# Mamba-2 scan and SwiGLU: additions of the states moved behind the preceding outputs, mean squares by one product, root by ScalarE, dummy products in the lead-in

## The chip, the cores and the metric

The kernel runs on one core of a Trainium2 chip. The metric is the device time of one execution in microseconds; lower is better. The engines named below are TensorE (PE, with its weight loads as PEld), VectorE (DVE), ScalarE (ACT), GpSimd (POOL) and SyncE (SP), which only issues transfers. Each engine works through its own list of instructions in order and waits at semaphores where it needs another engine's result.

## What is computed

A state-space scan over 32 sequences (4 batches of 8 heads, 768 tokens, 32 channels, 16 states) in chunks, and then a gated feed-forward layer over the 3072 tokens it gives. Cut to what matters:

```python
for c in range(nc):                      # chunks of a sequence
    cum = np.cumsum(log_a[:, :, sl], axis=-1)
    L = np.exp(cum[..., :, None] - cum[..., None, :]) * causal
    y_intra = einsum('bhij,bhjd->bhid', einsum('bhin,bhjn->bhij', Cc, Bc) * L, xc)
    y_inter = einsum('bhin,bhnd->bhid', Cc, state) * np.exp(cum)[..., None]
    y[:, :, sl] = y_intra + y_inter
    state = decay_full * state + sum_j(Bc_j (x) xc_j * decay_from_j)
x = y as (tokens 3072, features 256)
xn = x / np.sqrt(np.mean(x * x, axis=-1, keepdims=True) + 1e-06) * rms_g
g, val = xn @ w_gate, xn @ w_val         # (3072, 1536) each
out = (g / (1 + np.exp(-g)) * val) @ w_out
```

The weights arrive as 64-bit floats and are turned into 32-bit ones on the chip.

## The kernel before

**Tiling.** The tokens are cut into six blocks of 512 (`TB`), each of two pairs of 128-token chunks; a chunk has two halves of 64, which are the chunks of the scan. The scan is done by pairs (12 of them, index p), the feed-forward layer by blocks. The feed-forward products of blocks 1 to 5, and of part of block 0, are done by Strassen's scheme with seven half-size products in place of eight: `P.1` to `P.7` for gate and value, `O.1` to `O.7` for the output projection, with sums and differences by VectorE.

**A pair of the scan.** `turn` transposes B, C and the decayed C on TensorE (L464), `T` and `Tt` take them out of PSUM by ScalarE; `g` forms the products of C and B (L494) in a pair of PSUM banks, and `L`, `L1` multiply them by the decays (L513, L519). `scale` makes Cd and Bd on VectorE (L449). `A` (`additions`, L534) forms what each half chunk adds to the state, in tiles of 64 rows by 32 columns of the array, in two single banks of its own. `S` (`states`, L547 to L557) multiplies these by a mask of heads and adds them to the decayed state. `y` (`outputs`, L574) forms the outputs: first from the states, then from the decayed products. The outputs lie in columns 0 to 127 of four banks: the two of a pair of banks and two single ones. `sq` (L610, L613) squares them, and `yt` (L624, L626) takes them out.

**The norm of a block.** `ms` (L636) forms the mean squares of 4 x 128 tokens by four products with a 128x32 matrix, each in its own column tile of the array. `mc` (L642, ScalarE) copies them out, `mt` (L645) transposes them, so that a token has a partition; `rs` adds 1e-6 on VectorE (L650) and raises to the power -0.5 on GpSimd (L652). `rb` (L658) spreads the roots over all partitions by four transposes, into a bank from which `xn` (L670, VectorE) multiplies them with the outputs and the gain. `tx` (L754) forms differences of xn for Strassen's scheme.

**The feed-forward of a block.** For each j of six: `P.k.j` (L777) is two products of 128x256, into a bank "gate" (k = 1, 4, 6, 7) or "val" (2, 3, 5). The products of gate accumulate in one bank, and `take` (L783, ScalarE) copies its state p out between them: product 6 has to wait for the copy after product 1, and 4 or 7 likewise. `C` (L789, VectorE) adds p to val, `silu` (L798, ScalarE) and `hid` (L802, VectorE) make the hidden values. `O.k.j` (L867) is two products of 128x128; the products 1, 6 and 7 share a bank, of which `Otake` (L883, ScalarE) copies the state v out after each of the three, so that `O.6` waits for the first copy and `O.7` for the second. `Oadd` (L894) adds up, `out` stores. `s`, `s2`, `s3`, `s4` (L833 to L843) are the sums of hidden values.

**PSUM.** Single banks have the tag "one" and are two; the pair of banks for g and y is one from block 1 on (slot 2), and there are two "gate" and two "val".

**Order.** The kernel's work stands in one long string of some 1600 steps, `block:step.numbers`, written out by hand or by a planner outside of the file; the program goes through it and issues each step's instructions, which thus stand in this order on each engine. Nothing in the kernel shifts them. A step of block b concerns the scan of the block after it, or the second after it for loads (`when`, `of_pair`). ScalarE evaluates only functions of the table set that is loaded, and a load of another set (ACT_TABLE_LOAD) is put in where the next function needs it: Silu in the feed-forward, Exp for the decays (`ex`, L434). SP's queue carries the loads, the weights and the stores, in the order of the string.

**Lead-in.** Block 0 starts with the loads, constants, twelve dummy products of 128x256 (`idle`, L274), the sums of logarithms (`r`, `d`, `c`), the first two pairs of the scan and the change of the weights to 32 bits, twenty pieces of them (`pow` by ScalarE, L169 to L172, `man` and `wt` by VectorE, L179 to L188). The first products of block 0 (`early`, L703) are done on outputs that aren't normed yet.

Of the kernel before, what the change touches and what calls it, by code (L numbers as in the profile page):

```python
# [20 lines left out]
def kernel(  # L21
# [60 lines left out]

    def bank(name, shape):
        return mm.tile(list(shape), FP32, tag="one", bufs=2, name=name)

    def pair_of_banks(name, slot):
        return (mm if slot == 2 else pairs[slot].pool).tile([P, 2, 512], FP32, tag="pair%d" % slot, name=name)
# [108 lines left out]
    zeros = const.tile([P, P], FP32, name="zeros")  # L196
# [15 lines left out]
    mean32 = const.tile([P, 32], FP32, name="mean32")  # L212
    nhalf = const.tile([P, NT], FP32, name="nhalf")
# [79 lines left out]
    def both_mids():  # L293
# [9 lines left out]
        "zeros": lambda: nc.vector.memset(zeros, 0.0),  # L303
        "upto": lambda: triangle(upto, ones, 0.0, 0, 1),
        "never": lambda: triangle(never, zeros, -2.0 ** 100, 0, 1),
# [9 lines left out]
        "kinks": kinks_of_powers, "mean32": lambda: nc.vector.memset(mean32, 1.0 / DM),  # L315
        "nhalf": lambda: nc.vector.memset(nhalf, -0.5),
# [212 lines left out]
    def additions(p):  # L529
        s = st[p]  # L530
        ps["A", p] = A_ps = [bank("A_ps", (P, 2, 2, D)) for u in range(2)]
        for i, u in chunks_of(p)[2]:
            for q in range(NQ):
                nc.tensor.matmul(  # L534
                    out=A_ps[u][32 * q:32 * q + 32, i].rearrange("p t d -> p (t d)"),
                    lhsT=s["Bd"][halves[u], i, 2 * q:2 * q + 2].rearrange("p t n -> p (t n)"),
                    rhs=s["x"][halves[u], i, 2 * q:2 * q + 2].rearrange("p t d -> p (t d)"),
                    start=(i == 0), stop=True, tile_position=(HC * u, 32 * q),
                    skip_group_check=True)
# [24 lines left out]
    def outputs(p, y):  # L564
# [25 lines left out]
        for i in range(2):  # L590
            for h in range(NH):
                for u in range(2):
                    o = 32 * (h % 4)
                    product_y(h // 4, u, i, slice(o, o + 32), lhsT=s["x"][halves[u], i, h],
                              rhs=Ls[p][halves[u], i, h], tile_position=(HC * u, o))
        del st[p], Ls[p]
# [35 lines left out]
    def norm_sums(blk):  # L632

        ps["m", blk] = ms = bank("ms", (P, 2, P))
        for k in range(NT):
            nc.tensor.matmul(out=ms[32 * k:32 * k + 32, 0], lhsT=mean32,  # L636
                             rhs=sqs[blk][:, k * P:(k + 1) * P], start=True, stop=True,
                             tile_position=(0, 32 * k), skip_group_check=True)

    def norm_out(blk):  # L640
        ps["mr", blk] = mr = nrm.tile([P, P], FP32, tag="r_sb", name="mr", bufs=2)
        nc.scalar.copy(out=mr, in_=ps["m", blk][:, 0])  # L642

    def norm_back(blk):
        nc.tensor.transpose(out=ps["m", blk][:, 1], in_=ps.pop(("mr", blk)), identity=ident)  # L645

    def norm_roots(blk):
        me = nrm.tile([P, NT], FP32, tag="me", name="me")
        ms = ps.pop(("m", blk))[:, 1].rearrange("p (k r) -> p k r", r=32)[:, :, 0]
        nc.vector.tensor_scalar_add(me, ms, 1e-6)  # L650
        ps["rs"] = rs = nrm.tile([P, NT], FP32, tag="rs", name="rs")
        nc.gpsimd.tensor_tensor(out=rs, in0=me, in1=nhalf, op=ALU.pow)  # L652

    def norm_turn():
        rs = ps.pop("rs")
        ps["rb"] = rb = bank("rb", (P, NT, P))
        for k in range(NT):
            nc.tensor.transpose(out=rb[:, k], in_=rs[:, k:k + 1].to_broadcast([P, P]),  # L658
                                identity=ident)

    def norm_copy():
        ps["r"] = r = nrm.tile([P, TB], FP32, tag="sq2", name="r", bufs=1)
        nc.scalar.copy(out=r, in_=ps["rb"].rearrange("p k m -> p (k m)"))

    def norm_apply(blk):
        rb = ps["rb"].rearrange("p k m -> p (k m)")
        xns[blk] = nrm.tile([P, 2, TB], FP32, tag="xn", name="xn", bufs=1)
        if blk:
            for t in range(2):
                nc.vector.scalar_tensor_tensor(out=xns[blk][:, t], in0=yts[blk][:, t],  # L670
                                               scalar=gcol[:, t:t + 1], in1=rb,
                                               op0=ALU.mult, op1=ALU.mult)
        else:
            nc.vector.tensor_tensor(out=xns[0], in0=yts[0],
                                    in1=rb.unsqueeze(1).to_broadcast([P, 2, TB]), op=ALU.mult)
# [34 lines left out]
    def normed(f):  # L710
        gv = ps.pop(("gv", f))
        us[f] = ffn.tile([P, TB], FP32, tag="u", name="u", bufs=2)
        for k, dst in enumerate((us[f], of_block_0(f))):
            nc.vector.tensor_tensor(out=dst, in0=gv[:, k], in1=ps["r"], op=ALU.mult)
# [254 lines left out]
    def by_vector(out, in_, scale):  # L969
# [23 lines left out]
        "ms": norm_sums, "mc": norm_out, "mt": norm_back, "rs": norm_roots, "rb": lambda b: norm_turn(), "rc": norm_copy, "xn": norm_apply,  # L993
# [26 lines left out]
    def of_chunk(n, fn):  # L1020
# [18 lines left out]
        "ms": when(1, norm_sums), "mc": when(1, norm_out), "mt": when(1, norm_back),  # L1039
        "rs": when(1, norm_roots),  # L1040
        "rb": when(1, lambda b: norm_turn()), "xn": when(1, norm_apply), "tx": when(1, combine_x),
# [5 lines left out]
        0:a 0:bc.0 0:kinks 0:nhalf 0:ident 0:set 0:bc.1 0:warm 0:idle.12 0:fetch.1 0:fetch.0 0:x.0  # L1047
        0:head 0:mean32 0:x.1 0:gcol 0:zeros 0:never 0:ones 0:upto 0:upto2 0:mid 0:mid2 0:after
        0:after2 0:fetch.3 0:fetch.6 0:part 0:fetch.2 0:fetch.5 0:fetch.4 0:mids 0:never16 0:bc.2
        0:fetch.8 0:aT 0:la0 0:log4.6.2 0:log4.0.4 0:log 0:r.0 0:d 0:whole 0:x.2 0:ident16  # L1050
        0:mask.0/2 0:fetch.7 0:log4.4.2 0:part2 0:sel 0:parts.0 0:c 0:dx 0:turn.0.1 0:T.0.1 0:sums.0
        0:fetch.9 0:hmask 0:cx 0:tmask 0:Tt.0.1.1 0:Tt.0.1.0 0:turn.0.0 0:Tt.0.0.1 0:T.0.0
        0:turn.1.1 0:exp.0 0:Tt.0.0.0 0:g.0/10 0:T.1.1 0:Tt.1.1.0 0:Tt.1.1.1 0:turn.1.0 0:Tt.1.0.1
        0:T.1.0 0:Tt.1.0.0 0:scale.0 0:last.0 0:Tl.0 0:bc.3 0:row.1 0:scale.1 0:mask.1/2 0:sums.1
        0:L.0.1 0:cc 0:pow.0 0:L.0.0 0:rowout.1 0:man.1 0:A.0 0:exp.1 0:S.0 0:g.1/01 0:A.1 0:pow.1
        0:L.1.0 0:mask.3/2 0:S.1 0:y.0/0 0:pow.3 0:wt.1 0:L.1.1 0:sq.0 0:yt.0 0:ydone.0 0:pow.2
        0:r.1 0:man.0 0:last.1 0:parts.1 0:Tl.1 0:pow.5 0:y.1/1 0:wt.0 0:man.2 0:early.0.0/0 0:man.3
        0:sq.1 0:yt.1 0:ydone.1 0:pow.4 0:sums.3 0:scale.2 0:turn.2.0 0:mask.2/1 0:ms.0 0:wt.2
        0:sums.2 0:wt.3 0:man.4 0:fetch.16 0:mc.0 0:mt.0 0:rs.0 0:man.5 0:fetch.10 0:wt.4
        0:early.0.1 0:wt.5 0:exp.2 0:man.6 0:T.2.0 0:Tt.2.0.1 0:Tt.2.0.0 0:exp.3 0:turn.2.1 0:T.2.1  # L1060
        0:Tt.2.1.0 0:Tt.2.1.1 0:rb.0 0:rc 0:xn.0 0:norm.0 0:pow.6 0:fetch.13 0:wt.6 0:early.1.0/1
        0:early.1.1 0:silu.0 0:gg.2/2 0:norm.1 0:x.5 0:L1.2.2 0:gate.2/0 0:pow.7 0:man.7 0:hid.0
        0:row.0 0:man.8 0:silu.2 0:gate.3/1 0:pow.8 0:rowout.0 0:hid.2 0:scale.3 0:turn.3.0 0:x.3
        0:L1.2.3 0:wt.7 0:gate.4/0 0:wt.8 0:man.9 0:man.10 0:pow.9 0:wt.9 0:silu.3 0:hid.3 0:cw.3
        0:gate.5/1 0:silu.1 0:T.3.0 0:Tt.3.0.0 0:Tt.3.0.1 0:A.2 0:pow.10 0:tx.0 0:silu.4 0:hid.4
        0:switch.0 0:P.1.3 0:fetch.11 0:man.11 0:pow.11 0:S.2 0:turn.3.1 0:wt.10 0:take.1.3 0:P.6.3
        0:wt.11 0:P.1.4 0:Tt.3.1.0 0:L.2.0 0:silu.5 0:hid.5 0:fetch.19 0:fetch.12 0:man.12 1:bc.0
        0:man.13 0:T.3.1 0:Tt.3.1.1 0:pow.12 0:y.2/2 0:sq.2 0:x.4 0:yt.2 0:ydone.2 0:switch.1
        0:P.2.4 0:P.2.3 0:wt.12 0:A.3 0:S.3 0:gg.3/2 0:L.3.0 0:fetch.14 0:take.1.4 0:spread.10
        0:take.6.3 0:P.7.3 0:pow.13 0:fetch.15 0:L1.3.2 0:L1.3.3 0:y.3/2 0:sq.3 0:yt.3 0:ydone.3  # L1070
        0:C.11.3 0:P.5.3 0:cw.4 0:C.11.4 0:P.6.4 0:take.7.3 0:wt.13 0:P.5.4 0:pow.14 0:C.22.3 0:ms.1
        0:man.14 0:P.3.3 0:P.4.3 0:C.12.3 0:silug.22.3 0:wt.14 0:tok 0:silug.12.3 0:P.2.5
        0:silug.21.3 0:hidg.22.3 0:hidg.21.3 0:mc.1 0:o.0/2 0:take.6.4 0:P.7.4 0:P.1.5 0:hid.1 0:o.1
        0:man.15 0:pow.15 0:cw.5 0:wt.15 0:o.2 1:spread.2 0:pow.16 0:mt.1 0:man.16 0:wt.16 0:o.3
        0:hidg.12.3 0:take.1.5 0:P.6.5 0:take.7.4 0:C.22.4 0:P.3.4 0:bc.5 1:scale.1 0:fetch.17
        0:pow.17 0:man.17 0:C.12.4 0:o.4 0:o.5 0:tokout 0:sub.10 0:take.6.5 0:P.7.5 0:rs.1 0:rb.1
        0:silug.11.3 0:hidg.11.3 0:C.11.5 0:P.5.5 1:two.0 0:fetch.18 0:pow.18 0:wt.17 0:silug.11.5
        0:silug.11.4 0:hidg.11.4 0:man.18 0:wt.18 0:take.7.5 0:P.4.5 0:C.22.5 0:silug.21.5 0:man.19
        0:silug.12.4 0:hidg.12.4 0:P.4.4 0:silug.21.4 0:hidg.21.4 0:silug.22.4 0:hidg.22.4 0:o.6
        0:o.7 0:pow.19 0:wt.19 0:P.3.5 0:C.12.5 0:silug.12.5 0:o.8 0:o.9 0:silug.22.5 0:xn.1 1:P.2.1  # L1080
        1:P.1.1 1:P.2.0 1:take.1.1 0:ex.10 0:hidg.11.5 0:hidg.21.5 1:P.1.0 0:hidg.12.5 0:hidg.22.5
# [166 lines left out]
```

## Time and profile before

| what | value |
|---|---|
| device time, three runs | 414.24, 414.83, 415.03 us, median 414.83 |
| profiled execution | 414.91 us, of which the span from its first to its last instruction is 413.2 |
| HBM | 20.02 MB read, 3.28 MB written |
| busy, 0 to 50 us | TensorE 49.9, VectorE 41.8, ScalarE 37.1, GpSimd 6.3 |
| busy, 50 to 100 us | 49.6, 44.4, 35.0, 2.7 |
| busy, 100 to 206 us | 105.6, 81.1, 57.6, 15.3 |
| busy, 206 to 300 us | 93.4, 63.2, 44.2, 15.4 |
| busy, 300 to 413.2 us | 110.5, 70.5, 40.9, 2.7 |

The profile is a page on one execution: shares of busy time, the span in 40 slices, transfers, the chain of work that ended last, and groups of equal instructions. A line of a group, or of the timeline, names the source line, the engine, the operation, what it writes and reads, and shapes as partitions x elements. A 32-bit product appears as two records of TensorE, a transpose as one. Records of TensorE overlap, so that the distance between starts, not the duration of a record, is what one costs in a stream.

### The profile page before, as it was taken

What the parts mean: (1) busy time and instruction counts of PE and PEld (TensorE: products, weight loads), DVE (VectorE), ACT (ScalarE), POOL (GpSimd) and SP (SyncE); (2) the same over time, 40 slices, a digit from 0 to 9 for tenths busy, and PEclk for the clock granted to TensorE, in tenths of its full rate; (3) what the DMA queues carried; (4) which work ended last, traced back from release to release, by engine and by line L of the source; (5) the groups of instructions that cost most, each with busy time, mean ns of one, the idle gap of its engine ahead of it and who ended that gap; (6) DMA issues with size and microseconds to landing.
All of it is one profiled execution on the core that took longest, in us unless ns stands there. A gap on an engine that the chain in (4) does not pass through costs nothing.

```text
span 413.2 us, 10058 instructions
## 1 busy us (share of the span) xinstructions
PE 403.3 (98%) x4118; PEld 343.2 (83%) x4118; DVE 301.0 (73%) x712; ACT 214.8 (52%) x497; POOL 42.3 (10%) x64
## 2 busy tenths in 40 slices
PE   7789999999999999999999999999999999999997
PEld 5457467888888899888899888899988889988897
DVE  5989999789968878476796465787366876356781
ACT  2869997755656426645362547451556431235410
POOL 2011000012300015000033000012200001000000
PEclk9989999999999999999999999999999999999999
DMA  9979848900111440201070406000100000100001
GB/s 121 255 157 238 208 53 173 203 0 2 39 39 52 92 65 27 78 0 29 12 85 10 78 2 127 2 2 2 52 0 3 1 3 0 52 0 2 1 2 51
DMA packets 87374, 23.95 MB, mean 58 GB/s; under 512 B 76800, under 2 KB 81152, under 8 KB 87328
## 3 DMA queue, kind: packets, MB, share of 16 engines
q1 hardware_dynamic: 83168, 23.05, 26.9%
q10 hardware_dynamic: 4160, 0.26, 1.1%
q8 instruction: 32, 0.52, 0.5%
q14 instruction: 14, 0.11, 0.1%
HBM read 20.02 MB, written 3.28 MB: 56 GB/s over the span
## 4 chain that ended last, share of the span: by engine, by line
PE 90%; DVE 6%; issue 2%; ACT 1%; POOL 0%; DVEq 0%; POOLq 0%
PE gate L777 27%; PE o L867 21%; PE val L777 20%; PE y L574 4%; PE gate L693 3%; PE o L809 3%; PE gate L703 2%; PE g L494 2%; PE tp L464 1%; PE A_ps L534 1%; DVE sw L747 1%; PE rb L658 1%; PE idle L274 1%; DVE L L428 1%; PE ms L636 1%
## 5 line engine op out<-in xcount | busy, mean ns | idle before, releaser
L789 DVE TENSOR_TENSOR c<-val,p 128x512 f32<-128x512 f32 x99 | 67.5, 688 | 41.8 <-PE val L777 33.4
L783 ACT COPY p<-gate 128x512 f32<-128x512 f32 x99 | 57.6, 588 | 69.5 <-PE gate L777 67.6
L777 PE MATMUL gate<-tx,sw 128*128 128x256 f32 x264 | 66.8, 383 | 0.7 <-ACT p L783 0.7
L777 PEld LDWEIGHTS gate<-tx,sw 128*128 128x128 f32 x264 | 48.6, 190 | 8.5 <-ACT p L783 1.4
L798 ACT ACTIVATE c<-c 128x256 f32<-128x256 f32 x99 | 38.4, 417 | 24.6 <-DVE c L789 24.5
L802 DVE TENSOR_TENSOR h<-c 128x256 f32<-128x256 f32 x99 | 41.2, 429 | 10.9 <-ACT c L798 10.9
L777 PE MATMUL val<-tx,sw 128*128 128x256 f32 x132 | 34.1, 383 | 0.4 <-DVE c L789 0.4
L777 PE MATMUL val<-xn,wgv 128*128 128x256 f32 x132 | 33.7, 381 | 0.0
L777 PE MATMUL val<-xn,sw 128*128 128x256 f32 x132 | 33.5, 381 | 0.0
L777 PE MATMUL gate<-xn,wgv 128*128 128x256 f32 x132 | 33.1, 381 | 0.0
L777 PE MATMUL gate<-tx,wgv 128*128 128x256 f32 x132 | 33.0, 384 | 0.0
L613 POOL TENSOR_TENSOR sq<-sq 128x256 f32<-128x256 f32 x12 | 9.1, 760 | 213.6 <-ACT sq L610 187.5
L867 PE MATMUL o<-wo,h 128*128 128x128 f32 x240 | 30.8, 278 | 0.0
L867 PEld LDWEIGHTS o<-wo,h 128*128 128x128 f32 x240 | 28.6, 192 | 1.0 <-issue 0.6
L867 PE MATMUL o<-two,h 128*128 128x128 f32 x240 | 29.3, 275 | 0.0
L867 PE MATMUL o<-two,s 128*128 128x128 f32 x240 | 28.6, 275 | 0.0
L867 PEld LDWEIGHTS o<-two,h 128*128 128x128 f32 x240 | 28.1, 192 | 0.3 <-issue 0.2
L777 PEld LDWEIGHTS val<-tx,sw 128*128 128x128 f32 x132 | 24.5, 190 | 4.3 <-DVE c L789 0.8
L436 POOL TENSOR_SCALAR_AFFINE_SELECT L<-L 64x512 f32<-64x512 f32 x32 | 23.1, 722 | 47.4 <-ACT L L434 45.8
L867 PEld LDWEIGHTS o<-two,s 128*128 128x128 f32 x240 | 27.7, 192 | 0.0
L777 PEld LDWEIGHTS gate<-tx,wgv 128*128 128x128 f32 x132 | 24.5, 190 | 3.8 <-ACT p L783 0.2
L777 PEld LDWEIGHTS val<-xn,sw 128*128 128x128 f32 x132 | 24.7, 190 | 3.5 <-DVE m L179 0.2
(162 smaller groups left out, 651.4 us busy)
## 6 DMA issues: line engine op xcount, KB each, us to landing
L<-rowd SPq DMA_DIRECT2D x32, 128.0 KB, 3.8
xr<-in_x_dram SPq DMA_DIRECT2D x24, 128.0 KB, 4.4
wr<-in_moe_w_out_dram SPq DMA_DIRECT2D x6, 512.0 KB, 5.3
wr<-in_moe_w_gate_dram SPq DMA_DIRECT2D x5, 512.0 KB, 5.8
wr<-in_moe_w_val_dram SPq DMA_DIRECT2D x5, 512.0 KB, 6.9
out_dram<-ob SPq DMA_DIRECT2D x9, 256.0 KB, 2.2
br<-in_B_dram SPq DMA_DIRECT2D x22, 64.0 KB, 4.9
cr<-in_C_dram SPq DMA_DIRECT2D x22, 64.0 KB, 3.7
```

The costliest lines, as they stand in the source:

```text
L436: nc.gpsimd.affine_select(out=L[r], in_=L[r], pattern=[[0, NH], [1, HC]], compare_op=ALU.is_ge, fill=0.0, base=0, channel_multiplier=-1)
L494: nc.tensor.matmul(out=g[u, P * i:P * i + P].rearrange("p (t m) -> p t m", t=2), lhsT=T[r, i, 0, u], rhs=T[r, i, 1:3, u], start=(i == 0), ...
L574: nc.tensor.matmul(out=y[2 * k + u][rows, i * HC:(i + 1) * HC], start=(k, u, rows.start) not in opened, stop=True, skip_group_check=True, ...
L613: nc.gpsimd.tensor_tensor(out=sqs[blk][:, tk], in0=s2[:, 0], in1=s2[:, 1], op=ALU.add)
L693: nc.tensor.matmul(out=gv[:, k], lhsT=w[:, t, fs], rhs=xns[0][:, t], start=(t == 0), stop=(t == 1))
L777: nc.tensor.matmul(out=dst[:, half[w]], lhsT=lhsT, rhs=rhs, start=(k in (1, 2, 5) and w == 0), stop=True, skip_group_check=True)
L783: nc.scalar.copy(out=t, in_=Xs[j])
L789: nc.vector.tensor_tensor(out=t, in0=Zs[j], in1=a, op=ALU.add)
L798: nc.scalar.activation(out=u, in_=src[:, half[0]], func=AF.Silu)
L802: nc.vector.tensor_tensor(out=hidden_tile(blk, j)[:, c // 10 - 1, c % 10 - 1], in0=u, in1=src[:, half[1]], op=ALU.mult)
L809: nc.tensor.matmul(out=o, lhsT=hs_[blk, f // 2][:, f % 2, k // 2, (k % 2) * P:(k % 2 + 1) * P], rhs=wo[:, f], start=opens, stop=(f == NF - ...
L867: nc.tensor.matmul(out=o[t] if apart else o[:, t * P:(t + 1) * P], lhsT=lhsT[:, t], rhs=rhs, start=(k in (1, 2, 4, 5) and j == 0 and (apar ...
```

## The change

1. `additions` may be given banks. `outputs(p)` ends with the additions of pair p + 1, into columns 128 to 255 of the first two banks of its own outputs; the steps `A` of pairs 1 to 11 are gone, only `A.0` stays.
2. The mean squares of a block are one product of a 128x128 matrix of 1/256 with the squares, 128x512, so that each partition has the means of all tokens. `rs` is ScalarE's: Ln with a bias of 1e-6, then Exp with a scale of -0.5, into a tile r in SBUF (the buffer of the squares before their sum). `mc`, `mt`, `rb` and `rc` are gone; `xn` reads r.
3. A step may carry a number of dummy products, `*n`, of the bfloat16 tile `warm` with 256 columns, into the bank that the step takes first. Two do: `r.0*3` and `ms.0*2`.
4. `zeros` is no tile of its own any more.
5. The string of steps is another one throughout.

```diff
+    fillers = []
+    def filled(t, flat):
+        for k in range(fillers.pop() if fillers else 0):
+            nc.tensor.matmul(out=flat, lhsT=warm[:, 0:P], rhs=warm[:, 0:flat.shape[1]], start=True,
+                             stop=True)
+        return t
...
-    def additions(p):
+    def additions(p, A_ps=None):
         s = st[p]
-        ps["A", p] = A_ps = [bank("A_ps", (P, 2, 2, D)) for u in range(2)]
+        if A_ps is None:
+            A_ps = [bank("A_ps", (P, 2, 2, D)) for u in range(2)]
+        ps["A", p] = A_ps
...
+        if p + 1 < NPAIR:
+            additions(p + 1, [y[u][:, P:2 * P].rearrange("p (i t d) -> p i t d", i=2, t=2)
+                              for u in range(2)])
         del st[p], Ls[p]
...
-        ps["m", blk] = ms = bank("ms", (P, 2, P))
-        for k in range(NT):
-            nc.tensor.matmul(out=ms[32 * k:32 * k + 32, 0], lhsT=mean32,
-                             rhs=sqs[blk][:, k * P:(k + 1) * P], start=True, stop=True,
-                             tile_position=(0, 32 * k), skip_group_check=True)
-
-    def norm_out(blk):
...
-    def norm_back(blk):
...
+        ps["m", blk] = ms = bank("ms", (P, TB))
+        nc.tensor.matmul(out=ms, lhsT=mean, rhs=sqs[blk], start=True, stop=True)
 
     def norm_roots(blk):
-        me = nrm.tile([P, NT], FP32, tag="me", name="me")
-        ms = ps.pop(("m", blk))[:, 1].rearrange("p (k r) -> p k r", r=32)[:, :, 0]
-        nc.vector.tensor_scalar_add(me, ms, 1e-6)
-        ps["rs"] = rs = nrm.tile([P, NT], FP32, tag="rs", name="rs")
-        nc.gpsimd.tensor_tensor(out=rs, in0=me, in1=nhalf, op=ALU.pow)
-
-    def norm_turn():
...
-    def norm_copy():
...
+        ps["r", blk] = r = nrm.tile([P, TB], FP32, tag="sq2", name="r", bufs=1)
+        nc.scalar.activation(out=r, in_=ps.pop(("m", blk)), func=AF.Ln, bias=eps)
+        nc.scalar.activation(out=r, in_=r, func=AF.Exp, scale=-0.5)
```

The new string, where the turns of the blocks 0 to 1 and 2 to 3 stand:

```
0:o.6 0:o.7 0:o.8 0:silug.12.5 0:hidg.12.5 0:rs.1 0:cw.1 0:sub.11 0:ex.11 0:spread.8 0:sub.8
0:spread.9 0:sub.9 0:ex.9 0:ex.8 0:o.9 0:o.10 0:o.11 0:put.0 0:put.3 0:xn.1 0:tx.1 1:P.1.0
...
2:O.6.0 2:s4.0 2:yt.1 2:s3.3 2:sq.1 2:ms 2:rs 2:xn 2:tx 2:ex.0 2:O.6.1 2:O.6.2 2:O.6.3
2:O.6.4 2:s4.3 2:s4.1 2:s4.4 2:O.6.5 2:Otake.6 2:s4.5 2:s4.2 3:turn.0.1 3:T.0.1 3:Tt.0.1.0
3:Tt.0.1.1 3:turn.0.0 3:Tt.0.0.0 3:Tt.0.0.1 2:O.7.0 2:O.7.1 2:O.7.2 2:O.7.3 2:O.7.4 2:O.7.5
```

In the program as built, ScalarE's list has 26 table loads where it had 13: from block 1 on each `rs` has one ahead of Ln and one ahead of Exp, and Silu's follows.

## The prediction

> **What bounds the kernel.** I read the page first (busy shares, slices, chain), then the waits, then TensorE's timeline around the parts that change.
>
> ```profile
> span 413.2 us, 10058 instructions
> PE 403.3 (98%) x4118; PEld 343.2 (83%) x4118; DVE 301.0 (73%) x712; ACT 214.8 (52%) x497; POOL 42.3 (10%) x64
> PE   7789999999999999999999999999999999999997
> PEclk9989999999999999999999999999999999999999
> PE 90%; DVE 6%; issue 2%; ACT 1%; POOL 0%; DVEq 0%; POOLq 0%
> ```
>
> TensorE is busy 98% of the span and carries 90% of the chain: an instruction taken off it shortens the span unless another engine then comes late. The third slice's clock is below full. From TensorE's timeline (start, duration):
>
> ```profile
> 25.14 3.05 PE L703 MATMUL gate<-yt,wgv 128*128 128x256 f32 x8
> 31.07 1.89 PE L703 MATMUL gate<-yt,wgv 128*128 128x256 f32 x8
> ...
> 308.79 1.03 PE L777 MATMUL gate<-tx,sw 128*128 128x256 f32 x4
> 309.75 0.45 PE L534 MATMUL A_ps<-xr,Bd 64*32 64x64 f32 x32
> 310.13 1.13 PE L777 MATMUL val<-xn,wgv 128*128 128x256 f32 x4
> 311.10 1.03 PE L777 MATMUL gate<-tx,sw 128*128 128x256 f32 x4
> ...
> 336.23 1.50 PE L867 MATMUL o<-two,s 128*128 128x128 f32 x12
> 337.66 0.43 PE L636 MATMUL ms<-sq,mean 128*32 128x128 f32 x8
> 338.02 1.60 PE L867 MATMUL o<-wo,h 128*128 128x128 f32 x12
> 339.46 0.61 PE L867 MATMUL o<-two,h 128*128 128x128 f32 x4
> ```
>
> The same eight products take 3.05 us at 25 and 1.89 at 31: half clock. The other lines give prices by differences of start times. The chain's longest pieces give the steady pace: "45.42 7.00 PE gate L693 x16" is 0.437 us a record of 512 columns, 72 o records in 8.04 us are 0.112 each, eight gate records in 1.73 are 0.216. ScalarE enters through one kind of place:
>
> ```profile
> 235.92 1.28 ACT L1044 ACT_TABLE_LOAD   x1
> 237.22 0.42 ACT L798 ACTIVATE c<-c 128x256 f32<-128x256 f32 x1
> 237.54 0.57 ACT L783 COPY p<-gate 128x512 f32<-128x512 f32 x1
> ...
> 238.16 1.13 PE L777 MATMUL gate<-tx,sw 128*128 128x256 f32 x4 [0.39 <-ACT p L783]
> ```
>
> A table load delays the copy p, and TensorE, which adds into the bank that p reads, starts 0.55 us late (236.63 + 0.32 + 3 x 0.216 = 237.60 was due). Stalls of this kind after 50 us are few: 0.5 at 54.5, 0.55 at 108.7, 0.55 here, 0.4 at 225 (rb waits for GpSimd's root).
>
> **What the skill says.** "TensorEngine Tiling (Array Packing)", Key Properties: changing the tiling mode drains TensorE, changing the tile does not. The trace agrees: between two full-array records the start distance is 0.216, from a full-array to a tiled one it is 0.309. "TensorE: Matmul & The Clock Gate", Part 1: after about 3.4 us of idleness the clock is halved, and comes back after a busy window; the 20 to 30 us window of the trace has a mean clock of 0.83, which is 3.4 us at half. "ScalarE: Activation LUTs", What ACT_TABLE_LOAD costs: 1283 ns and about 1380 of drain at each switch; the trace has the 1283, but an ACTIVATE starts 0.02 us after the load (above), so I charge 1.28 only. The same page, Table sets, has Ln and Exp together in one set; the changed program as built nevertheless loads one set for Ln and another for Exp from block 1 on.
>
> **The change, part by part.**
>
> State additions. Around the one shown: from 308.79 to 311.10 are 2.31 us for eight records worth 1.73, so the excursion costs 0.58. Its 32 records themselves stream for 0.24 (start times 7 to 8 ns apart). Behind the outputs of the preceding pair they share that group's tiles of 64 x 32, and its exit is paid once: 0.58 - 0.24 = 0.34 saved. Ten of the twelve stand alone after 50 us (pairs 2 to 11); one of those is followed by another tiled group and saves less: 10 x 0.34 - 0.2 = 3.2 us. Pair 1's lies in the lead-in, where TensorE waits anyhow: 0. The price is that Bd and x of the next pair, half a block earlier, must be there; the order puts scale and the loads well ahead, so 0. The two small vector reads of the additions now hold the pair of banks of y; they come first after y, ahead of yt and sq, and the next group of products needs the pair only after 2.6 us or more. They no longer take both single banks. "PSUM — Partial Sum Buffer", The four PSUM rules, has that a start flag clears a bank's written bits and not its data, so y's values in columns 0 to 127 survive; no run shows it.
>
> Mean squares. Before, per block: ms 336.23 to 339.46 is 3.23 for 24 o records worth 2.69, 0.54; one transpose (mt) 0.11; four (rb) 0.44: 1.09. After: one 128x512 product, two records, 0.875. Saved 0.215 x 5 = 1.1, block 0 in the lead-in aside. The wait for GpSimd's root, 0.4, goes. VectorE loses me (0.16 a block), GpSimd 1.07 a block: both off the path, 0.
>
> ScalarE. Ln and Exp of 128x512: 0.63 each by the nearest row (L434, 128x512, 626 ns), twelve of them 7.5; table loads 13 before, 26 after, 13 x 1.28 = 16.7; less the copies mr and r (2.2): +22 us on 215 of 413. The average leaves room; the places decide. What waits behind it is the copy v of the o bank (O.7 adds into the bank that v reads) and xn. The load for Ln waits for nothing, so it runs before ms is there; after ms come Ln 0.63, load 1.28, Exp 0.63, then v 0.37.
> - Block 1 to 2: 2.9 us against O.6, three O.4 and two turns on TensorE, 4.7: hidden.
> - 2 to 3: an ex (0.63) stands in between, 3.5 us and 0.2 of handing over, against five O.6 (2.24) and two turns (0.66), 2.9: 0.8 late.
> - 3 to 4: v, ex, two loads, Ln, Exp and half of xn, 5.5, against fourteen O products, 6.3: hidden.
> - 4 to 5: v, 3.8 and 0.7, 4.9, against twelve, 5.4: hidden.
> Cost +0.8. Bounds: 0, and 5 x 1.28 = 6.4 if every turn shows one load more than I count. Loads amid the gate phase (one extra for ex.10) are priced by 238.16 at 0.55; the old stalls of that kind, 1.6 in sum, go or come with the new order: net 0, between -1.6 and +1.6.
>
> Head. Three dummy products ahead of r stand in a wait (r_ps starts at 5.73, 0.98 idle); 3 x 0.21 fit, at 0, else +0.6. The two ahead of ms cost up to 0.4, I take 0.2. They may keep the clock up: the half-clock stretch costs 3.4 / 2 = 1.7, and whether a window is busy enough I can't read from the trace of before; I take half, -0.85. Sum -0.65. The order of the head is new throughout. By xn of block 1 VectorE has now 5.9 us more behind it (two weight combinations 2.9, four h products 1.35, a scale 0.67, states 1.3, two subtractions more 1.3, less one combination 1.5 and me); TensorE has 2.6 more (two o steps 1.73, two turns 0.66, additions 0.24) and saves 0.9. TensorE would ask for xn at 96.1 + 1.7 - 0.85 = 97; VectorE gives its first half at 93.4 + 5.9 + 0.75 = 100, less what it recovers of its idle time (13.7 us before xn in before, of which 2.0 for ms, 2.3 and 0.95 later on are waits that a new order can fill). I take 97 and 0; bounds 0 and +2.9.
>
> Tail: the same last projection half, sum and store: 0.
>
> Sum against the profiled execution, 414.91 (span 413.2 and 1.7 around it): -3.2 - 1.1 - 0.4 + 0.8 - 0.65 = -4.55, 410.4; the median of the runs is 0.1 lower, so 410.3.
>
> **Rivals.**
> A, slower: ScalarE is late at the block turns. The place is v and xn behind Ln, load and Exp; the price a load of 1.28 shown at each of five turns, 6.4 in place of 0.8: 415.9. It decides once the turns cost 1.1 each, 5.4 in all. For it: the margins above are 0.5 to 1.8 us and ScalarE has work ahead of the load that I may have placed too early; the load at 235.92 did reach TensorE. Against: ScalarE is idle 48%, and waits for o products 39.5 us in total at just these turns (row of v among the waits). 0.30.
> B: VectorE binds the head, xn of block 1 is 2.9 late: 413.2. For it: VectorE is 90 to 98% busy between 30 and 60 us. Against: its waits listed above. 0.14.
> C: the clock never drops and the wait of 1.5 us at 21.7 (r_ps for yt) goes with the new order: 410.3 - 0.85 - 1.5 = 407.9. 0.11.
> D: the change doesn't do what it says: the additions drain between outputs and themselves as they did alone, 3.2 fall away: 413.5. Both have the form 64*32, which speaks against it. 0.05.
> My sum: 0.40, own range 408.8 to 412.
>
> **How the numbers follow.** A change within 0.2%, 0.8 us, is one that a measurement of this kernel can't tell from none. Faster: my sum, C, and nearly all of B and D, 0.68; slower: A with the most of its chance, 0.27; same 0.05 from the edges of A, B and D. Range: 407.4 leaves out half of C, 416.4 the upper third of A.
>
> **What would show it.** Right: additions follow y at TensorE with no 0.3 us step and no 1.13 us gate group of their own; ms two records of 0.43; the table loads 26; the third slice's clock at 9. Wrong: TensorE below 97% busy, its waits naming ACT v, ACT p or DVE xn with more than 3 us; o records after ms more than 1 us late in several blocks; a gap before the first gate product of block 1.

## Result, and the profile after

The changed kernel takes 427.26 us (median of four runs, 425.68 to 428.51) beside 414.53 for the kernel before: a ratio of 1.031, 95% interval 1.026 to 1.037. It is slower by 12.7 us where 410.3 was forecast. The profiled execution is the one of 425.68 us, with a span of 423.7, so 10.5 us of span are to be found.

The page of the changed kernel: span, busy shares, slices of TensorE, clock and DMA, and the chain.

```profile
span 423.7 us, 9941 instructions
PE 402.8 (95%) x4057; PEld 343.2 (81%) x4057; DVE 301.5 (71%) x706; ACT 238.1 (56%) x515; POOL 35.8 (8%) x58
PE   6668998999999999899998999999999999999997
PEclk9977999999999999999999999999999999999999
DMA  9972989404023401505300350100100000000001
PE 49%; DVE 6%; ACT 1%; issue 0%; POOL 0%; DVEq 0%
```

TensorE is busy for as many microseconds as before, but for 95% of the span instead of 98%. In the first 50 us it is busy for 38.1 us, where the kernel before has 44.2 (its table above says 49.9, which its trace doesn't bear out). The slices say where: the first four (0 to 42 us) read 6, 6, 6, 8, where the kernel before has 7, 7, 8, 9. The clock is at 7 in slices three and four, where before the third alone was at 8. The DMA engines are at 2 in the fourth slice, where the kernel before has 9. Of the later slices of TensorE three read 8 instead of 9. The chain can be followed back over 57% of the span only, so it isn't used here.

What TensorE waited for in the changed kernel (total, times, longest):

```profile
PE tp L476 <- ACT early L384: 4.7, 1, 4.7
PE y L588 <- DVE yt L643: 2.1, 1, 2.1
PE y L548 <- DMA rowd<-r_sb: 1.8, 1, 1.8
...
PE o L861 <- ACT v L877: 0.6, 1, 0.6
```

The three largest lie before 34 us. The last line is the place at the turn from block 2 to 3 that the prediction named.

A ledger from the starts of TensorE's records: "work" is the number of records of each form times the median distance from such a record to the next start; "rest" is stalls, changes of tiling and half clock. The cut is the first product of block 1 into a gate bank that reads its xn (`P.1`; in the order of the kernel before a `P.2` of 0.86 us stands ahead of it).

| us, profiled executions | before | changed | a1_bc1 | c1_fetch | d1_c1_oneset | b1_join | b6_split |
|---|---|---|---|---|---|---|---|
| up to the cut | 96.9 | 109.1 | 105.3 | 104.3 | 101.5 | 97.0 | 96.1 |
| work in it | 76.1 | 80.6 | 80.2 | 80.6 | 78.2 | 76.0 | 75.5 |
| rest in it | 20.9 | 28.5 | 25.1 | 23.6 | 23.3 | 21.0 | 20.6 |
| after the cut | 316.3 | 314.6 | 313.8 | 314.4 | 312.5 | 330.2 | 315.5 |
| work in it | 294.3 | 291.9 | 291.9 | 291.9 | 291.9 | 294.3 | 294.3 |
| rest in it | 21.9 | 22.7 | 22.0 | 22.6 | 20.6 | 35.9 | 21.2 |

So of the 10.5 us, 7.6 are rest of the head, 0.8 rest after it, and 2.1 more work: dummy products 0.9, and 1.3 because ten full records of 0.43 replace sixty-five small ones (what that saves in changes of tiling stands in the row "rest"). The remainder of the 4.5 in the head's work row was moved there from later. The medians are each execution's own, so slow records of the head count as work too: c1_fetch and d1_c1_oneset have the same head, and differ by 2.8 us up to the cut, 2.4 of it in the row "work" (the last section says why). The rows of the head are good to that much and no better.

The head's largest stall, from the timelines of ScalarE and then of TensorE (start, duration, what ended the idle time; ACTq is ScalarE's own queue issuing a transfer):

```profile
10.09 0.38 ACTq L121 DMA_DIRECT2D br<-in_B_dram  x1
11.77 0.37 ACTq L121 DMA_DIRECT2D cr<-in_C_dram  x1
12.19 0.49 ACT L384 ACTIVATE early<-full_ps 128x384 f32<-128x384 f32 x1 [6.57 <-DMA wr<-in_moe_w_val_dram]
```

```profile
6.49 1.49 PE L379 MATMUL full_ps<-la,chunk_ones 128*128 128x192 f32 x4
12.73 0.47 PE L476 MATMUL tp<-ident,br 128*128 128x128 f32 x1 [4.75 <-ACT early L384]
```

L384 reads a bank that TensorE's next transposes need. Its input was ready at about 8 us, yet it ran at 12.19, because two loads of B and C for pair 1 stand ahead of it in ScalarE's list, and each of those could be issued only when an older transfer had landed, at 10.07 and 11.74 us (the trace has eight landing semaphores, which the transfers take in turn, each waiting for the last one on its own). In the kernel before these loads stand near the head of the list and were issued at 1.95 and 4.17. The step bc.1 had been moved behind the logs.

### The profile page after: what moved, and what is told of

It is laid out like the page before. It is cut to its first block, busy times and chain, and to the rows that moved or that the text cites. A ratio compares the mean times of both kernels' runs of the same rounds, so it can differ in the third digit from the quotient of the medians.

```text
span 423.7 us, 9941 instructions
## 1 busy us (share of the span) xinstructions
PE 402.8 (95%) x4057; PEld 343.2 (81%) x4057; DVE 301.5 (71%) x706; ACT 238.1 (56%) x515; POOL 35.8 (8%) x58
## 4 chain that ended last, share of the span: by engine, by line
PE 49%; DVE 6%; ACT 1%; issue 0%; POOL 0%; DVEq 0%
PE gate L771 18%; PE val L771 14%; PE o L861 13%; PE y L588 2%; DVE h L831 1%; DVE h L796 1%; DVE s L827 1%; PE tp L476 1%; PE ms L652 1%; PE g L506 1%; DVE S L571 1%; DVE tx L748 0%; DVE xn L664 0%; PE y L548 0%; DVE s L837 0%
## 5 line engine op out<-in xcount | busy, mean ns | idle before, releaser
L792 ACT ACTIVATE c<-c 128x256 f32<-128x256 f32 x99 | 40.4, 418 | 34.8 <-DVE c L783 34.6
L861 PE MATMUL o<-two,s 128*128 128x128 f32 x240 | 29.6, 276 | 1.2 <-DVE s L834 1.2
L861 PE MATMUL o<-wo,h 128*128 128x128 f32 x240 | 29.8, 277 | 0.0
L771 PEld LDWEIGHTS val<-xn,wgv 128*128 128x128 f32 x132 | 24.7, 190 | 3.9 <-issue 0.6
```

The source lines that it names most:

```text
L771: nc.tensor.matmul(out=dst[:, half[w]], lhsT=lhsT, rhs=rhs, start=(k in (1, 2, 5) and w == 0), stop=True, skip_group_check=True)
L792: nc.scalar.activation(out=u, in_=src[:, half[0]], func=AF.Silu)
L861: nc.tensor.matmul(out=o[t] if apart else o[:, t * P:(t + 1) * P], lhsT=lhsT[:, t], rhs=rhs, start=(k in (1, 2, 4, 5) and j == 0 and (apar ...
```

## Experiments

All ratios are to the kernel before on the same chip, with 95% intervals.

**a1_bc1: the loads of pair 1 early.**

```diff
-  0:bc.0 0:ident ... 0:never16 0:bc.1 0:fetch.2
+  0:bc.0 0:bc.1 0:ident ... 0:never16 0:fetch.2
```

> The changed kernel with one step of the head moved: the loads of B and C of pair 1 (bc.1) are issued directly after those of pair 0, as the kernel before has it, instead of behind the logs. Theory (head order): two of these four loads stand in ScalarE's own queue and hold up the copy L384, which TensorE's first transposes wait for; the wait of 4.75 us at 12.7 us goes, and the time falls by 4 to 5 us, from 427 to about 422.5, a ratio of about 1.02 to the kernel before. Rival (VectorE or the transfers bind the head, and the wait only comes later): 0 to -1 us, ratio 1.03.

Measured: 422.08 us, ratio 1.019 (1.014 to 1.024): 5.2 us less than the changed kernel in the medians and 4.5 between the profiled executions, as the theory said. ScalarE and TensorE in its trace:

```profile
8.56 0.49 ACT L384 ACTIVATE early<-full_ps 128x384 f32<-128x384 f32 x1 [2.40 <-PE full_ps L379]
```

```profile
9.11 0.47 PE L476 MATMUL tp<-ident,br 128*128 128x128 f32 x1 [0.58 <-ACT early L384]
```

The copy now waits for its own data and TensorE for 0.58 instead of 4.75. A moved transfer cost some 5 us through the queue that it was issued on, while its own data were not late at all.

**a2_oneset: one table load per root.**

```diff
+        if blk:
+            nc.scalar.preload_act_table_set("natural_log_exp_and_others")
         nc.scalar.activation(out=r, in_=ps.pop(("m", blk)), func=AF.Ln, bias=eps)
```

> The changed kernel with one table load in place of two for each root of blocks 1 to 5 (the set that has Ln and Exp together is loaded by hand ahead of Ln): 21 loads in place of 26. Theory (head order): the loads mostly lie beside other work; only the 0.6 us wait of o for v at 232 us and little else goes, -0.5 to -1.5 us. Rival (ScalarE late at the block turns, the prediction's case A): each turn gains a load of 1.28, -4 to -6.4 us, ratio about 1.017.

Measured: 425.04 us, ratio 1.025 (1.024 to 1.027), 2.2 below the changed kernel: a little over the upper edge of the theory and far from the rival. Its timeline of ScalarE at the turn from block 2 to 3, after that of the changed kernel:

```profile
229.64 1.28 ACT L657 ACT_TABLE_LOAD   x1
230.93 0.63 ACT L657 ACTIVATE r<-r 128x512 f32<-128x512 f32 x1
231.47 0.61 ACT L446 ACTIVATE L<-L 128x512 f32<-128x512 f32 x1
231.99 0.35 ACT L877 COPY v<-o 128x256 f32<-128x256 f32 x1
```

```profile
230.66 0.63 ACT L659 ACTIVATE r<-r 128x512 f32<-128x512 f32 x1
231.19 0.61 ACT L446 ACTIVATE L<-L 128x512 f32<-128x512 f32 x1
232.17 0.37 ACT L879 COPY v<-o 128x256 f32<-128x256 f32 x1 [0.36 <-PE o L863]
```

Exp follows Ln without the load of 1.28, and v, which stood ready behind it before, now waits for TensorE: the stall of 0.61 there is gone. After the cut the profiled execution is 1.5 us shorter than that of the changed kernel.

**a3_nofill: no dummy products.**

```diff
-  0:r.0*3 ... 0:ms.0*2
+  0:r.0 ... 0:ms.0
```

> The changed kernel without its five dummy products (three ahead of r, two ahead of ms of block 0). By the prediction's term (dummies worth 0.65): +0.65 us. Theory now[...]: -0.2 to +0.2 us, ratio 1.030.

Measured: 427.65 us, ratio 1.030 (1.026 to 1.035); the changed kernel's is 1.031. The dummies do nothing that can be measured. They stand at 4.6 and 38.2 us, and in the changed kernel's trace the clock stands at half from 26.5 to 36.7. It fell ahead of the stalls that end at 29.3 and 33.1, not behind them.

**b1_join: the first part alone, in the order of the kernel before.**

```diff
+        if 5 <= p + 1 < NPAIR:
+            additions(p + 1, [y[u][:, P:2 * P].rearrange(...) for u in range(2)])
-  1:y.0 ... 1:A.1 ... 1:S.1 1:y.1
+  1:y.0 1:S.1 ... 1:y.1
```

> The kernel before with the first part of the change alone, and only where the order needs least: the additions of pairs 5 to 11 join the outputs of pairs 4 to 10, each state update directly behind them; x of pair 6 and B, C and the scaling of pair 8 stand earlier so that they are there. The head is that of the kernel before. By the prediction's term: 7 x 0.34 = -2.4 us, 412.2, ratio 0.994. Rival (the bank pair is held for the additions, so that squares and copies of y come late and VectorE's state updates come at a bad time): the saving on TensorE is eaten, 0 to +2 us, ratio 1.000 to 1.005.

Measured: 429.19 us, ratio 1.037 (1.034 to 1.040), 14.7 us slower: both expectations missed, in the direction of the rival and seven times its size. All of it lies after the cut, in the row "rest". VectorE and TensorE around one of its stalls:

```profile
212.63 0.42 DVE L549 TENSOR_TENSOR A<-y,tmask 128x128 f32<-128x128 f32 x2 [4.61 <-PE y L536]
212.97 0.92 DVE L559 SCALAR_TENSOR_TENSOR S<-S,fcol,A 128x64 f32<-128x64 f32 x3
213.80 0.42 DVE L807 TENSOR_TENSOR h<-c 128x256 f32<-128x256 f32 x1
214.32 0.69 DVE L794 TENSOR_TENSOR c<-val,p 128x512 f32<-128x512 f32 x1
```

```profile
215.07 2.07 PE L782 MATMUL val<-xn,sw 128*128 128x256 f32 x4 [2.48 <-DVE c L794]
216.94 1.58 PE L782 MATMUL gate<-tx,wgv 128*128 128x256 f32 x4
```

VectorE's next instruction was the read of the joined additions; TensorE had not got there, and VectorE idled for 4.61 us with h and c ready behind it. Then, with TensorE waiting for c, VectorE did the reads and the state update first. The stall of 2.48 us drew 1.6 more behind it: groups of four such records, 1.03 elsewhere, take 2.07 and 1.58, at half clock (0.50 from 215 to 218).

**b5_late: the state step three VectorE steps later.**

```diff
-  1:y.0 1:S.1 1:sq.0 ... 1:C.22.4 1:P.3.4
+  1:y.0 1:sq.0 ... 1:C.22.4 1:S.1 1:P.3.4
```

> b1_join with the state updates three VectorE steps later in the order, behind the sums and products that TensorE asks for next, rather than directly behind the outputs. Theory (in b1_join VectorE stood waiting for the joined additions, and its update of 1.8 us came ahead of a sum that TensorE waited for; the stalls of over 2 us then halve the clock): most of the +14.7 us goes, time 413 to 417, ratio 0.997 to 1.006. Rival (the held banks, or the steps moved for pairs 6 and 8, cost it): +8 us or more stay.

Measured: 422.05 us, ratio 1.018 (1.014 to 1.022). Half of the cost went: less than the theory asked for (417 at most), more than the rival (+8 or more) allowed. TensorE's waits for c and p, six of 0.4 to 1.7 us, stayed.

**b6_split: short reads behind the outputs, long updates at their old place.**

```diff
+    def reads(p): ...        # A_ps.pop, new = additions * tmask
     def states(p):
+        new = ps.pop(("new", p))
-  1:y.0 1:S.1 ... 1:y.1          (as in b1_join)
+  1:y.0 ... 1:two.4 1:Sr.1 1:g.1 ... 1:silu.22.5 1:S.1 1:x.0 1:y.1
```

> The kernel before with the additions of pairs 5 to 11 joined as in b1_join, and the state step split: only the two short reads of the additions (0.5 us) stand behind the outputs, six VectorE steps later or just ahead of the next products that take the bank pair, and the state updates (1.8 us) stay where the kernel before has them. Theory (the join costs because VectorE waits for the joined additions with other work behind it, and because its long update then comes ahead of sums that TensorE asks for): the cost of b1_join (+14.7) and of b5_late (+6.9) goes, and what the trace of the changed kernel shows as saved by a join, 0.2 for each of 7, remains: 412.5 to 414.5, ratio 0.995 to 1.000. Rival (the bank pair being held, or x and B, C of pairs 6 and 8 earlier, is the cost): 419 or more.

Measured: 413.63 us (20 runs), ratio 0.9974 (0.9950 to 0.9998): 0.9 us faster than the kernel before, with an interval that just leaves out 1, as the theory said. VectorE behind an output of the same pair as above:

```profile
203.68 0.69 DVE L800 TENSOR_TENSOR c<-val,p 128x512 f32<-128x512 f32 x1 [0.70 <-ACT p L794]
204.29 0.41 DVE L549 TENSOR_TENSOR A<-y,tmask 128x128 f32<-128x128 f32 x2
204.62 0.41 DVE L813 TENSOR_TENSOR h<-u,gate 128x256 f32<-128x256 f32 x1
```

The reads wait for nothing here, and h and c are not held up. The join and the held bank pair are the same as in b1_join; the place of VectorE's waiting instruction and of its long update made the difference of 15 us. Which of the two weighs more isn't shown: b5_late moves both to one place, b6_split to two. After the cut the profile is 0.8 us shorter than before, of some 2 that seven joins should save; a wait for p of 0.95 at 236.9, where before has 0.39, took a part back. This version is the fastest of all that ran.

**b2_norm and b7_normlate: the second part alone, in the order of the kernel before.**

```diff
-  1:ms 1:mc ... 1:mt 1:rs ... 1:rb ... 1:xn
+  1:ms 1:rs ... 1:xn          (b2_norm: Ln and Exp where mc stood)
+  1:ms ... 1:rs ... 1:xn      (b7_normlate: where rs stood; one set)
```

> The kernel before with the second part of the change alone: one product for the mean squares, root by Ln and Exp on ScalarE (24 table loads in place of 13), at the place in the order where the copy of the sums stood; the rest of the order and the head are those of the kernel before. By the prediction's terms: -1.1 - 0.4 + 0.8 = -0.7 us, 413.8, ratio 0.998. Rival (ScalarE late at the block turns): +2 to +6 us, ratio 1.005 to 1.015.

> The kernel before with the new norm alone, with one table load ahead of Ln in place of two, and Ln and Exp at the place of the old root instead of that of the old copy (in block 3 ahead of the Exp of the decays). Theory (in b2_norm three to four loads in a row, Ln and Exp stand ahead of the copies p and v and of SiLU at the block turns): of the +9.4 us of b2_norm 5 to 8 go, 415 to 419, ratio 1.002 to 1.010. By the prediction's terms, with the loads halved: -1.5 us, 413, ratio 0.996.

Measured: b2_norm 423.9 us, ratio 1.024 (1.019 to 1.029), more than even the rival said; b7_normlate 417.86, ratio 1.012 (1.004 to 1.020), as its theory. ScalarE in b2_norm:

```profile
281.19 1.28 ACT L639 ACT_TABLE_LOAD   x1
282.48 0.63 ACT L639 ACTIVATE r<-r 128x512 f32<-128x512 f32 x1
283.13 1.28 ACT L774 ACT_TABLE_LOAD   x1
284.42 0.72 ACT L774 ACTIVATE c<-c 128x256 f32<-128x256 f32 x2
285.16 1.28 ACT L433 ACT_TABLE_LOAD   x1
```

With a fourth load at 279.10, four loads take 5.1 of 7.4 us; behind them VectorE waits for a SiLU (c) and TensorE for VectorE's h, 1.9 us. The prediction's rival A is a real mechanism; the changed kernel's own order avoids most of it. In neither place did the norm alone gain.

**a6_oldnorm: the changed kernel with the old norm.**

```diff
-  1:ms 1:rs ... 1:xn
+  1:ms 1:mc 1:mt 1:rs ... 1:rb 1:xn
```

> The changed kernel with the norm of the kernel before put back (tiled mean squares, copy, transposes, GpSimd's root), its steps beside those that they replace; joined additions, head order and dummies stay. By the prediction's terms the old norm costs 1.1 + 0.4 - 0.8 = +0.7 us. Rival (Ln, Exp and the doubled table loads are what eats the gain after block 1, 4 us of stalls there): -2 to -4 us.

Measured: 439.84 us, ratio 1.061 (1.056 to 1.066), 12.6 slower than the changed kernel. Both expectations missed. With root and rb close together TensorE waited for GpSimd four times, 1.4 us each, and for xn behind it. It tells little of what the new norm is worth; it tells, as b1_join and b2_norm do, that a step of one norm in a place that was arranged for the other costs more than the step.

**a5_sepA1: the additions of pair 1 on their own.**

```diff
-  0:A.0 0:S.0 ... 0:y.0/2 ... 0:S.1 0:sq.0
+  0:A.0 0:S.0 0:A.1 0:S.1 ... 0:y.0/2 ... 0:sq.0      (on a1_bc1)
```

> The changed kernel with the loads bc.1 early as in a1_bc1, and the additions of pair 1 on their own, with their state update, ahead of the outputs of pair 0; the other joins stay. Theory (the join in the head makes a chain outputs of pair 0, additions, state update of pair 1, outputs of pair 1, with TensorE idle for 2.3 us and at half clock behind it): -2.5 to -4 us against a1_bc1, about 418.5, ratio 1.009. Rival (that stall is a late copy yt, whatever the additions do, or the fetching of TensorE's instructions): 0 to -0.5 us.

Measured: 422.98 us, ratio 1.021 (1.016 to 1.025): no gain on a1_bc1. The stall ahead of y.1, 2.1 us in a1_bc1's trace, is gone, so it was the join's, but other waits came up: 0.53 for the separate additions, and later 1.97 for c, at a time when VectorE had waited 3.3 us for weights.

**c1_fetch and c2_sepA_fetch: two weight loads ahead of the store of the row sums.** Between 30 and 40 us the DMA engines of the changed kernel stand at a share of 0.07, those of the kernel before at 0.93. SyncE's queue says why:

```profile
27.55 0.99 SPq L128 DMA_DIRECT2D xr<-in_x_dram  x2
38.80 0.37 SPq L942 DMA_DIRECT2D rowd<-r_sb  x1
39.22 0.97 SPq L160 DMA_DIRECT2D wr<-in_moe_w_gate_dram  x2
```

For 10 us it held a store that waits for VectorE, with the weights behind it.

```diff
-  0:row.0 ... 0:rowout.0 ... 0:fetch.6 ... 0:fetch.8
+  0:fetch.6 0:fetch.8 0:row.0 ... 0:rowout.0
```

> a1_bc1 with two weight loads (pieces 6 and 8) issued ahead of the row sums and their store instead of behind them. In a1_bc1 the queue of SyncE stands for 9 us (26 to 35 us) at the store, which waits for VectorE, and all later loads wait behind it; the DMA engines move next to nothing. Theory (VectorE then waits for weights, 0.8 to 2 us, and TensorE for VectorE): -1 to -3 us against a1_bc1 (422.1), about 420, ratio 1.014. Rival (VectorE has 6.6 us more work ahead of xn of block 1, and that alone binds): 0 to -0.5 us.

> a5_sepA1 (additions of pair 1 on their own) with the same two weight loads ahead of the store. In a5_sepA1 VectorE waited 3.3 us for weights between 37 and 107 us and TensorE stood 1.97 us at 73. Theory (the late weights took back what the additions on their own had gained): -3 to -5 us, about 418.5, ratio 1.009. Rival: as a5_sepA1, 423, ratio 1.020.

Measured: c1_fetch 419.78 us, ratio 1.014 (1.008 to 1.020), 2.3 below a1_bc1 as expected; VectorE's wait for weights in that stretch is 0.1 us. c2_sepA_fetch 420.89, ratio 1.016 (1.010 to 1.023): 2.1 below a5_sepA1, less than the theory's 3 to 5. The runs of c1_fetch and a1_bc1 overlap, those of c2_sepA_fetch and a5_sepA1 don't. The late weights were a cost; that they hid a gain of the separate additions was wrong.

**d1_c1_oneset and d2_split: what is left.**

```diff
 c1_fetch
+  one table load per root               (d1_c1_oneset)
+  0:y.0/2 ... 0:Sr.1 0:sq.0 0:exp.3 0:yt.0 0:S.1      (d2_split, and so for all pairs)
```

> c1_fetch (the changed kernel with bc.1 and two weight loads earlier) and one table load for each root, as in a2_oneset. If the loads are a cost of their own: -1.5 to -2.5 us against c1_fetch (419.8), 417.5 to 418, ratio 1.008. If the 2 us of a2_oneset were head time that c1_fetch has back already: 0 to -0.5.

> d1_c1_oneset with the state step split for pairs 1 to 11 as in b6_split: the reads of the joined additions stay behind the outputs, the state updates come some VectorE steps later (in the head behind the copies yt, which TensorE's next outputs wait for). If VectorE's updates behind the outputs are a cost in this order too: -1 to -3 us against d1_c1_oneset, the wait of 2.3 us at 29 shrinks to about 1. If this order was arranged around them: 0 to +2 us.

Measured: d1_c1_oneset 418.48 us (20 runs, 415.89 to 422.14), ratio 1.010 (1.007 to 1.012), 1.3 below c1_fetch in the medians; after the cut, where its loads are, 1.9 less in the profiles. d2_split 419.98, ratio 1.013 (1.007 to 1.018): the wait at y.1 fell from 2.5 to 1.0, and new ones of up to 0.9 came after the cut. The order of the changed kernel was arranged around its updates; moving them there gains nothing.

In the medians: 5.2 us are bc.1, 2.3 the weights behind the store, 1.3 the second table load. Each of the last two steps is within the spread of its own runs; that they are costs rests also on the other pair of runs for each (c2_sepA_fetch against a5_sepA1, a2_oneset against the changed kernel). Of the 4.0 left, the changed kernel's column of the ledger has 2.1 as more work; the other 1.9 were not taken apart further and stay open. The chain y.0, additions, update, y.1 with half clock behind it is in it, but no run removed it with a net gain.

## Why the prediction was wrong

- **The head** is the step that failed most: "TensorE would ask for xn at 96.1 + 1.7 - 0.85 = 97 ... I take 97 and 0". It asked at 109: by the ledger 4.5 us of more records (1.7 forecast, though some of the 4.5 is half speed) and 7.6 of stalls and half clock (-0.85 forecast). The prediction noted that the order of the head was new throughout and then priced only VectorE's added work (5.9; measured 6.6, its busy time up to xn of block 1 being 86.3 us after 79.7) and the dummies. It didn't walk the two queues that issue transfers: bc.1 on ScalarE's (5.2 us) and the weights behind a store on SyncE's (2.3 us). Rival B named the engine and not the mechanism: TensorE waited 0.2 us for xn.
- **Half clock.** The term of -0.85 had the wrong sign. From 25 to 40 us the mean granted clock (third from the right in the lines below) is 0.65, 0.50 and 0.83 by fives, in total some 10 us at half against 3.4 before:

```profile
25.00:30.00 5.00, 3.18 (x161) 2.34 (x164) 2.59 (x10) 2.75 (x4) 0.00 (x0) 0.65 0.79 232
30.00:35.00 5.00, 2.91 (x129) 2.44 (x133) 4.64 (x13) 3.06 (x7) 0.72 (x1) 0.50 0.08 13
```

  Nor was its cause as stated: no stall of 3.4 us stands in the 10 us ahead of the fall in either trace (the longest are 1.50 us before and 0.89 in the changed kernel). The dummies were worth 0 (a3_nofill): of the -0.65 for dummies and clock together nothing came.
- **State additions, saving.** Right in kind, somewhat large. In the changed kernel's trace the outputs alone and with joined additions, up to the start of the second group of full records behind them:

```profile
329.65 0.69 PE L588 MATMUL y<-T,S 32*64 32x64 f32 x32
...
330.93 0.44 PE L548 MATMUL y<-xr,Bd 64*32 64x64 f32 x22
331.30 1.13 PE L771 MATMUL val<-xn,wgv 128*128 128x256 f32 x4
332.27 1.03 PE L771 MATMUL gate<-tx,sw 128*128 128x256 f32 x4
```

```profile
341.82 0.69 PE L588 MATMUL y<-T,S 32*64 32x64 f32 x32
...
344.19 1.03 PE L771 MATMUL val<-xn,sw 128*128 128x256 f32 x4
```

  2.62 against 2.37: 24 joined records cost 0.25, and 32 (at 148.77) 0.32. Alone they cost 0.55 and 0.58, so a join saves 0.28 rather than 0.34; 2.8 us for ten. There is no step between outputs and additions: rival D is out. (The expectation of b6_split says 0.2; it left the slower first record behind the group out.)
- **State additions, price.** "The two small vector reads ... needs the pair only after 2.6 us or more" asked only who needs the bank, and cost it at nothing. What counts is what stands behind the waiting read on VectorE and ahead of the next sum: +14.7 us in b1_join, -0.9 with the update elsewhere (b6_split). In the changed kernel, by the waits of VectorE, it stands for the reads of the joined additions eight times, and in block 0 the reads and the update stand ahead of yt, for which y.1 waits 2.1 us:

```profile
DVE A L561 <- PE y L548: 8.1, 8, 2.4
```

  The longest, 2.4, is TensorE's own: it stood for 1.82 us just ahead of these additions (last section).

- **Mean squares.** Two records a block, 1.02 us as a pair at 227.87, and GpSimd's wait of 0.4 is gone, as computed.
- **ScalarE.** 26 loads and 23.3 us more (22 forecast). The late v at the turn from 2 to 3 cost 0.61 where 0.8 was worked out, by the very sequence given. Rival A's price of 6.4 did not come: one load less per root is worth 1.3 to 2.2.
- **After the cut** TensorE did save what was forecast: seven joins at 0.28 and four tiled mean squares at 0.48 (0.54 less 0.06 of work) are about 4 us of "rest". The row grew by 0.8 all the same, so nearly 5 us of new losses stand there. Stalls of more than 0.12 us are 3.1 of them: they rose from 1.0 to 4.1, with 1.25 at 179 (a copy T behind a decay), 0.65 and 0.51 for s, 0.61 for v, 0.68 for p and 0.30 for c. The rest was not located. "The old stalls ... go or come with the new order: net 0" was the second assumption that failed, by some 3 us.
- **Tail**: 0 was right. From the last product into gate or val to the end are 21.88 us in both.

## What to carry to other kernels

Where an order is written out by hand, walk a moved step through every list that it issues on, its transfers' queues included: what stands behind it there waits for what it waits for. Before two pieces of work are joined to save TensorE a change of mode, look at the engine that reads the result: split the read that frees the bank from the long update, and put each where that engine would not stand still. And a stall can cost more than its length: some 1.6 us more behind that of 2.48 us in b1_join, where 3.4 us at half clock followed. In these runs the length alone doesn't tell when: stalls of 2.29 us (b1_join) and 1.97 us (a5_sepA1) were followed by half clock as well, stalls of 2.14 us (b2_norm, at 74.9) and 1.98 us (b1_join, at 151) were not.

## What the runs showed that was not expected

- TensorE may run out of instructions. In the head of every profile with the order of the changed kernel (ten of them) a stall of 0.5 to 3.2 us ends at the same place in its instruction stream (the 693rd to 695th record, weight loads counted), 1.2 to 1.5 us behind the landing of a packet of 16 KB on the DMA queue that the page calls "instruction". In the changed kernel it is the 1.82 us that end at 29.3 (put down to a store; the loads of x that these additions need had landed by 20.5). In TensorE's timeline of a5_sepA1 it splits a group of outputs that had been running:

```profile
23.77 0.67 PE L588 MATMUL y<-L,xr 64*32 64x64 f32 x31
26.11 0.74 PE L588 MATMUL y<-L,xr 64*32 64x64 f32 x33 [1.67 <-issue]
```

  The records of one group stand on both sides of 1.67 us in which the trace shows nothing to wait for. That it is the fetching of instructions is read from these traces; no run was made to settle it. The stall of 1.5 us at 21.7 in the kernel before isn't of this kind: it is for yt, as its page and the prediction have it.

```profile
20.94 0.99 DVE L626 TENSOR_SCALAR yt<-y,gcol 128x256 f32<-128x256 f32 x3
21.73 0.70 PE L331 MATMUL r_ps<-mids,la 128*128 128x256 f32 x2 [1.50 <-DVE yt L626]
```

  In all six profiles with that order it ends 0.05 to 0.06 us behind the second of the three records of yt, whether a packet landed up to 0.5 us earlier or up to 0.3 us later.
- The first products of the span run at half speed, and for how long differs between executions. The views show a granted clock of 1.00 there, but only for want of a record: the trace's first record of the clock, at full, stands at 4.5 us in d1_c1_oneset, 10.2 in the kernel before, 12.8 in c1_fetch and 16.2 in the changed kernel. The same pair of products in c1_fetch and in d1_c1_oneset:

```profile
5.99 1.19 PE L343 MATMUL r_ps<-mids,la 128*128 128x256 f32 x2 [0.61 <-ACT la L300]
```

```profile
6.08 0.67 PE L343 MATMUL r_ps<-mids,la 128*128 128x256 f32 x2 [1.02 <-ACT la L300]
```

  By 16 us the first was 2.6 us behind the second, with the same instructions. It may be why the runs of d1_c1_oneset spread over 6 us; the profiled one, 416.02, is near their lower end.
- The clock changes in steps. Every recorded stretch at half that a later one at full ends lasted 3.41 us or 2, 3, 4 or 5 times that: 3.42 in the kernel before, 10.24 in the changed one, 6.83 in d1_c1_oneset, 13.66 in c2_sepA_fetch, 17.06 in a2_oneset.
